# DMA chains that add up weight blocks, put at other steps of a kernel of attention and two feed-forward blocks

## The chip, the core and the metric

The kernel runs on one core of a Trainium2 chip. The metric is the device time of one execution in microseconds (us); lower is better. The engines are named as the profile names them: PE is TensorE, DVE is VectorE, ACT is ScalarE, POOL is GpSimd, SP is SyncE, which here only issues DMAs.

## What is computed

Attention over 4 batches and 12 heads, and then two feed-forward blocks on its 1792 tokens of width 768. All is float32 in the result; the five weight matrices arrive as float64.

```python
def _attn_ref(q, k, v, g_q, g_k):            # (4, 12, 448, 64)
    q_n, k_n = rmsnorm(q, g_q), rmsnorm(k, g_k)
    scores = 1.0 / np.sqrt(64) * np.matmul(q_n, k_n.transpose(0, 1, 3, 2))
    ...                                      # softmax over the keys
    return np.matmul(attn, v)

x = attn_out.transpose(0, 2, 1, 3).reshape(1792, 768)
h = 1.0 / (1.0 + np.exp(-(x @ w_gate))) * (x @ w_val)     # 768 -> 1536
y = h @ w_out                                             # 1536 -> 768
r = np.maximum(y @ w_in2, 0.0)                            # 768 -> 2048
out = (r * r) @ w_out2                                    # 2048 -> 768
```

## The kernel before

A batch is 448 tokens. The kernel has four stretches. A prologue does the attention of batch 0. **The first sweep** runs the four layers (gate and value; `w_out`; `w_in2`; `w_out2`) for batch 0 while the attention of batch 1 is done between its matmuls; in it the weights are read as float64, made float32 and written back to DRAM as blocks `w32[i]` (named `w` in the rows, 128 x 768). **The second sweep** runs the four layers for batch 1, and between them goes the attention of batches 2 and 3, twelve pairs of heads. **The joint stretch** runs the four layers for batches 2 and 3 together. Its first, third and fourth layers do a product of 2 x 2 blocks with seven block products in place of eight (`seven`), which needs sums of the blocks of the weights beside the blocks themselves.

Every weight block is loaded from DRAM into one of three buffers `wraw` (L143, L149, issued by SP), and split into a high and a low part `wsp` (four buffers) by an ACT cast (L193) and a DVE subtraction (L194); a float32 product is then three matmuls (`mm3`).

**The sums of the weights** are made by DMAs alone, in DRAM. `add_up` (L594) makes one sum in two halves: SP copies the first term to its place (L599), and later POOL adds the second term to it with an accumulating DMA (L597). A chain is three stages of such sums, in all four copies and four accumulations of 192 KB each, where a later stage copies a result of an earlier one. `pair_chains` makes the chains of the first layer (tiles `ws`, 12 chains) and of the third (tiles `wu`, 8 chains), `quad_chains` those of the fourth (tiles `wt`, 8 chains). `set_out(at, chains_, first, apart, gap)` is the table that puts them in time: half `h` of stage `n` of chain `i` is issued at step `first + apart * i + gap * (2 * n + h)`. In the second sweep a step is one of the pieces, some 2 us long, into which the sweep is cut (the sweep yields after each); in the joint stretch it is a beat, one block product of nine matmuls in the first and third layers. The joint stretch has 84 beats in the first layer, 24 in the second and 56 in the third, and whatever stands at a later beat is issued at the end of the third layer (`beat_on(30)`).

**The attention of a pair of heads in the second sweep** takes 16 or 17 pieces and starts while the pair before it is being finished: its q and k are loaded (L381, SP); DVE sums their squares (L255) and scales the sums (L260); POOL raises them to the power -1/2 (L261); DVE multiplies q and k by the result (L265, tile `qk`); PE turns them (L571, `att<-ident,qk` or `acc<-ident,qk`); ACT and DVE split them into `ks` and `qs` (L414, L415, L422, L425); SP moves halves of `qs` and `ks` to other partitions (L434, then L430); and only then can PE compute the scores (L566, `att<-ks,qs`). Behind them come the row maxima (L447), the turned probabilities (L479, L487, L491, tile `parts`) and the product with v (L566, `att<-parts,vs`). The last pieces of the sweep also split parts of the joint stretch's input (`x_part`, L638 on ACT and L639 on DVE).

PE's instructions are held in program order in these two stretches, and SP, POOL, DVE and ACT each work through one list in order. The order of those lists is made by the framework's scheduler from the program order, by its own model of time. So a step moved in the table can change the order of other instructions too. A copy or an accumulation of a chain is tied in that order to the matmul ahead of it, but does not wait for it on the chip: it waits only for its data.

Of the kernel before, what the change touches and what calls it, by code (L numbers as in the profile page):

```python
# [17 lines left out]
def attention_moe_moe2_kernel(  # L18
# [20 lines left out]
    K1 = F1 // 128  # L39
    K2 = F2 // 128  # L40
# [59 lines left out]
    K4 = K2 // 2  # L100
# [3 lines left out]
    w1s = [dram_p.tile([128, 1536], F32, tag=f"ws{p}", name=f"ws{p}") for p in range(K1)]  # L104
    w3s = [dram_p.tile([128, 1536], F32, tag=f"wu{p}", name=f"wu{p}") for p in range(K2 // 2)]
# [15 lines left out]
    W3 = 2 * K1 + 2 * KD  # L121
# [479 lines left out]
    def set_out(at, chains_, first, apart, gap):  # L601
        for i, chain in enumerate(chains_):
            for n, sums in enumerate(chain):
                for half in range(2):
                    at.setdefault(first + apart * i + gap * (2 * n + half), []).append((add_up, (sums, half)))

    beat, at_beat = [0], {}
# [7 lines left out]
    def pair_chains(i0, i1, t):  # L615
        a11, a12, a21, a22 = (w32[i][:, h:h + 384] for i in (i0, i1) for h in (0, 384))
        s = [t[:, 384 * n:384 * (n + 1)] for n in range(4)]
        return [[(s[0], a21, a22), (s[2], a11, a21)], [(s[1], s[0], a11)], [(s[3], s[1], a12)]]

    def quad_chains(kb):  # L620
        b11, b21, b12, b22 = (
            w32[W4 + K4 * hf + kb][:, 384 * r:384 * r + 384] for hf in range(2) for r in range(2))
        t = [wt[n][kb // 2][:, 384 * (kb % 2):384 * (kb % 2) + 384] for n in range(4)]
        return [[(t[0], b11, b12), (t[2], b12, b22)], [(t[1], t[0], b22)], [(t[3], t[1], b21)]]
# [76 lines left out]
    def joint():  # L701
        edge = att_tile()
        for kc in range(NF + 1):
            n = 128 if kc < NF else TAIL
            nc.tensor.transpose(edge[:n, 0, kc * QR:(kc + 1) * QR], ident[:QR, :n], ident[:QR, :QR])
        set_out(at_beat, [quad_chains(kb) for kb in range(K4)], 4, 14, 10)
        hr = one.tile([128, 27, N], F32R, tag="hr", name="h")
        rt = one.tile([128, 9, N], F32R, tag="rt", name="h")
        room = [hr[:, i] for i in range(27)] + [rt[:, i] for i in range(9)]
# [580 lines left out]
    next(pro, None)  # L1290
    def steps_of_1():
        at = {}
        set_out(at, [pair_chains(4 * (p // 2) + p % 2, 4 * (p // 2) + 2 + p % 2, w1s[p]) for p in range(K1)]
                + [pair_chains(W3 + 2 * m, W3 + 2 * m + 1, w3s[m]) for m in range(K2 // 2)], 5, 8, 8)
        order.extend(["xy1", "raw64", "raw64", "raw64", "kq", "qs", "kq", "p", "p", "pt", "p"])
        for j in range(3):
            for i, what in enumerate(("B11", "B21")):
                at.setdefault(158 + 6 * j + 3 * i, []).append((x_part, (j, what)))
        for i, what in enumerate(("sums", "B22")):
            at.setdefault(180 + 4 * i, []).append((x_part, (0, what)))  # L1300
            at.setdefault(195 + 3 * i, []).append((x_part, (1, what)))
        return at

    for s in range(2):
        slots = slots_of(s + 1)
        if s == 0:
            xtile[1] = xbuf(1)
        else:
            xwhole[0] = one.tile([128, 2, KD, N], F32, tag="xy0", name="xwhole")
        total, done = len(slots), 0  # L1310
        extra = steps_of_1() if s == 1 else {}
        for i, _ in enumerate(sweep(s)):
            if s == 0 and i == 0:
                for _ in pro:
                    pass
                continue
            fixed[0], roomy[0] = s == 1, s == 1 and i < 150
            now[0] += 1
            tick()
            for fn, args in extra.pop(i, []):  # L1320
                fn(*args)
            want = min(total, i + 1 if s == 1 else (i + 1) * total // 66)
            while done < want:
                for f in slots[done]:
                    f()
                done += 1
# [7 lines left out]
    for _ in joint():  # L1334
        pass
# [30 lines left out]
```

## Time and profile before

| what | value |
|---|---|
| median of 3 runs | 1268.12 us (1268.11 to 1270.33) |
| the profiled execution, its own time | 1264.9 us |
| span in the trace, first to last instruction | 1263.1 us |
| mean granted clock of TensorE | 0.996 of full |
| busy: PE, DVE, ACT, POOL | 98%, 75%, 63%, 18% of the span |
| second sweep and joint stretch, in the trace | about 390 to 811 us, and 811 to 1263 us |

Busy times are shares of the span; a busy PE isn't PE at its peak, since a matmul that runs at half clock is busy too. Idle time ahead of an instruction stands in brackets behind it, with what ended it.

### The profile page before, as it was taken

How to read it: one execution, taken by the hardware profiler on the slowest of the kernel's cores; microseconds unless marked ns; L12 is line 12 of the kernel's file. 1: busy time of each engine (PE TensorE's matmuls, PEld its weight loads, DVE VectorE, ACT ScalarE, POOL GpSimd, SP SyncE). 2: the span in 40 equal slices, each digit the busy share in tenths (PEclk: the TensorE clock that was granted, in tenths of full speed). 3: DMA queues.
4: the chain of work that ended last, by engine and by line, in shares of the span. 5: the costliest groups of instructions: out<-in, count | busy, mean ns of one | idle time of the engine just before them, and what ended most of it. 6: DMA issues, size and time to landing. Idle time of an engine off the chain costs nothing.

```text
span 1263.1 us, 19134 instructions
## 1 busy us (share of the span) xinstructions
PE 1234.6 (98%) x6599; PEld 1079.7 (85%) x6599; DVE 946.4 (75%) x1492; ACT 791.9 (63%) x1603; POOL 228.6 (18%) x236
## 2 busy tenths in 40 slices
PE   8999999999999999999999899999999999999998
PEld 6545788878888988898887898999999999999998
DVE  6866988778875788987887766777886336889872
ACT  5757886768765887876788665666564323335451
POOL 3301323211220222333333221001111000000000
PEclk9999999999999999999999899999999999999999
DMA  5535998998796688899899745355665334543443
GB/s 138 129 122 151 312 324 263 296 285 239 234 321 174 168 180 193 211 218 227 201 218 215 164 108 140 115 151 148 170 174 145 76 91 111 137 124 94 133 137 114
DMA packets 200545, 225.81 MB, mean 179 GB/s; under 512 B 83968, under 2 KB 178176, under 8 KB 200448
## 3 DMA queue, kind: packets, MB, share of 16 engines
q1 hardware_dynamic: 177024, 175.36, 48.1%
q0 software_dynamic: 21568, 48.77, 17.5%
q8 instruction: 52, 0.85, 0.3%
q10 hardware_dynamic: 1856, 0.46, 0.2%
q14 instruction: 45, 0.37, 0.1%
HBM read 185.99 MB, written 76.28 MB: 208 GB/s over the span
## 4 chain that ended last, share of the span: by engine, by line
PE 86%; DVE 4%; ACT 3%; DMA 3%; issue 2%; SPq 1%; POOL 0%; DVEq 0%; ACTq 0%; POOLq 0%
PE acc L566 54%; PE att L566 17%; PE att L291 3%; PE att L571 3%; DMA ks<-ks 2%; PE acc L345 2%; PE att L345 1%; PE acc L914 1%; PE acc L327 1%; PE att L327 1%; PE acc L571 1%; DVE wsp L194 1%; ACT p L458 1%; DMA out_dram<-ob 0%; ACT wsp L193 0%
## 5 line engine op out<-in xcount | busy, mean ns | idle before, releaser
L566 PE MATMUL acc<-xy,wsp 128*128 128x448 f32 x1368 | 304.9, 373 | 4.8 <-ACT wsp L193 2.7
L193 ACT CAST wsp<-wraw 128x768 fp32r<-128x768 f32 x246 | 205.8, 837 | 160.1 <-PE acc L566 72.2
L194 DVE TENSOR_TENSOR wsp<-wraw,wsp 128x768 fp32r<-128x768 f32 x246 | 235.5, 958 | 85.9 <-ACT wsp L193 83.8
L566 PEld LDWEIGHTS acc<-xy,wsp 128*128 128x128 f32 x1368 | 252.1, 189 | 35.8 <-ACT wsp L193 5.4
L566 PE MATMUL att<-parts,wsp 128*128 128x448 f32 x720 | 152.4, 365 | 0.0
L566 PEld LDWEIGHTS att<-parts,wsp 128*128 128x128 f32 x720 | 135.2, 188 | 10.8
L566 PE MATMUL acc<-parts,wsp 128*128 128x448 f32 x540 | 116.0, 365 | 0.0
L261 POOL TENSOR_TENSOR ms<-ms,mhalf 112x16 f32<-112x16 f32 (+1 forms) x25 | 81.8, 3273 | 186.6 <-DVE ms L260 174.5
L566 PE MATMUL acc<-wsp,rb 128*128 128x384 f32 x576 | 110.3, 341 | 0.0
L566 PEld LDWEIGHTS acc<-parts,wsp 128*128 128x128 f32 x540 | 101.4, 188 | 8.0
L566 PEld LDWEIGHTS acc<-wsp,rb 128*128 128x128 f32 x576 | 100.8, 190 | 2.4 <-issue 1.3
L566 PE MATMUL acc<-hb,wsp 128*128 128x448 f32 x432 | 95.1, 371 | 0.0
L566 PE MATMUL acc<-h,wsp 128*128 128x448 f32 x432 | 87.7, 365 | 0.0
L566 PEld LDWEIGHTS acc<-hb,wsp 128*128 128x128 f32 x432 | 79.3, 188 | 9.2 <-issue 2.8
L566 PEld LDWEIGHTS acc<-h,wsp 128*128 128x128 f32 x432 | 81.2, 188 | 6.4
L597 POOL DMA_DIRECT2D wt<-w x32 | 26.2, 860 | 288.8 <-DMA wt<-wt 208.3
L167 ACT ACTIVATE wraw<-raw 128x768 f32<-128x768 f32 x64 | 58.4, 914 | 27.7 <-DVE wsp L194 15.7
L182 POOL DMA_DIRECT2D w<-wraw x64 | 35.6, 556 | 205.6 <-DVE wraw L175 194.0
L458 ACT ACTIVATE p<-att,nm 112x448 f32<-112x448 f32 x96 | 60.0, 631 | 16.1 <-DVE nm L447 15.0
L309 ACT ACTIVATE p<-att,nm 112x448 f32<-112x448 f32 x88 | 55.2, 638 | 21.3 <-DVE nm L297 19.5
L566 PE MATMUL acc<-wsp,rp 128*128 128x384 f32 x360 | 64.0, 334 | 0.0
L566 PEld LDWEIGHTS acc<-wsp,rp 128*128 128x128 f32 x360 | 62.6, 188 | 0.0
(205 smaller groups left out, 2041.7 us busy)
## 6 DMA issues: line engine op xcount, KB each, us to landing
wraw<-w SPq DMA_DIRECT2D x80, 384.0 KB, 3.8
w<-wraw POOLq DMA_DIRECT2D x64, 384.0 KB, 6.3
raw<-in_moe_w_out_dram SPq DMA_DIRECT2D x28, 768.0 KB, 7.1
wraw<-w SPq DMA_DIRECT2D x92, 192.0 KB, 2.5
raw<-in_moe_w_in_dram SPq DMA_DIRECT2D x16, 768.0 KB, 5.9
raw<-in_moe_w_gate_dram SPq DMA_DIRECT2D x12, 768.0 KB, 6.4
raw<-in_moe_w_val_dram SPq DMA_DIRECT2D x12, 768.0 KB, 6.5
ws<-w POOLq DMA_DIRECT2D x48, 192.0 KB, 5.8
```

What stands on the lines that cost most here:

```text
L167: size = nc.scalar.activation(out=t, in_=hi.bitcast(F32), func=AF.Prelu, scale=2.0 ** -112, alpha=2.0 ** 32)
L182: nc.gpsimd.dma_start(out=w32[i], in_=wraw[i])
L193: nc.scalar.copy(out=sp[:, 0], in_=t)
L194: nc.vector.tensor_tensor(out=sp[:, 1], in0=t, in1=sp[:, 0].bitcast(F32), op=ALU.subtract)
L261: nc.gpsimd.tensor_tensor(out=ms, in0=ms, in1=mhalf[:QR, 0:ms.shape[1]], op=ALU.pow)
L291: nc.tensor.matmul(out=ps[:QR, e, :S], lhsT=kq[a, 1, c * QR:(c + 1) * QR], rhs=kq[a, 0], start=True, stop=True)
L309: nc.scalar.activation(out=p[:, e], in_=ps[:QR, e, :S], func=AF.Exp, bias=nm[:, e:e + 1], scale=st["rq"][:, c, e:e + 1] if "rq" in st else ...
L345: nc.tensor.matmul(out=o[e * D:(e + 1) * D], lhsT=v[:, kc, e], rhs=pt[:, (NF + 1) * e + kc if kc < NF else NF], start=(kc == 0), stop=(kc ...
L458: nc.scalar.activation(out=p[:, i * S:(i + 1) * S], in_=ps[:QR, i, :S], func=AF.Exp, bias=nm[:, i:i + 1], accum_out=su[:, c, e:e + 1])
L566: m = latest[0] = nc.tensor.matmul(**kw)
L571: m = nc.tensor.transpose(*a)
L597: held(nc.gpsimd.dma_start(out=dst, in_=second, accum_op=ALU.add))
```

## The change

Three calls of `set_out` are put differently. The eight chains of the third layer leave the second sweep, where they stood behind the twelve of the first layer, and go to the beats 2 to 104 of the joint stretch. The twelve chains that stay in the sweep begin 13 steps apart in place of 8, so that the last half stands at step 188 in place of 197 (which was a third-layer chain's). The eight chains of the fourth layer begin at beat 60 in place of 4, 13 apart in place of 14, with halves 5 beats apart in place of 10; their last half stands at beat 176 in place of 152, which is behind the 164 beats of the first three layers. No instruction is added or dropped.

```diff
@@ joint
-        set_out(at_beat, [quad_chains(kb) for kb in range(K4)], 4, 14, 10)
+        set_out(at_beat, [pair_chains(W3 + 2 * m, W3 + 2 * m + 1, w3s[m]) for m in range(K2 // 2)], 2, 11, 5)
+        set_out(at_beat, [quad_chains(kb) for kb in range(K4)], 60, 13, 5)
@@ steps_of_1
-        set_out(at, [pair_chains(4 * (p // 2) + p % 2, 4 * (p // 2) + 2 + p % 2, w1s[p]) for p in range(K1)]
-                + [pair_chains(W3 + 2 * m, W3 + 2 * m + 1, w3s[m]) for m in range(K2 // 2)], 5, 8, 8)
+        set_out(at, [pair_chains(4 * (p // 2) + p % 2, 4 * (p // 2) + 2 + p % 2, w1s[p]) for p in range(K1)], 5, 13, 8)
```

PE's list is the same in both kernels; the lists of the other engines differ at the places where chains stand, and at a few more. Three of them follow.

On DVE, in the second sweep where its fourth layer begins, the two multiplications L265 that scale q and k of the eleventh pair stand near the splits L639 of the joint stretch's input and the copies L487 and L491 of the probabilities. Before:

```order
817 L194 TENSOR_TENSOR wsp<-wraw,wsp 128x768
818 L639 TENSOR_TENSOR parts<-xwhole,parts 128x448 x3
819 L447 TENSOR_REDUCE nm<-att 112x2
820 L639 TENSOR_TENSOR parts<-xwhole,parts 128x448 x3
821 L487 TENSOR_TENSOR parts<-att,parts 128x3x224
822 L491 TENSOR_TENSOR parts<-att,parts 64x112 x2
823 L265 TENSOR_TENSOR qk<-qk,ms 112x512 x2
824 L194 TENSOR_TENSOR wsp<-wraw,wsp 128x768
```

With the change:

```order
817 L194 TENSOR_TENSOR wsp<-wraw,wsp 128x768
818 L639 TENSOR_TENSOR parts<-xwhole,parts 128x448 x3
819 L447 TENSOR_REDUCE nm<-att 112x2
820 L265 TENSOR_TENSOR qk<-qk,ms 112x512 x2
821 L639 TENSOR_TENSOR parts<-xwhole,parts 128x448 x3
822 L487 TENSOR_TENSOR parts<-att,parts 128x3x224
823 L491 TENSOR_TENSOR parts<-att,parts 64x112 x2
824 L194 TENSOR_TENSOR wsp<-wraw,wsp 128x768
```

The two L265 have moved ahead of three L639, one L487 and two L491.

On SP, in the second sweep at the fifth pair of heads, where the halves of `qs` and `ks` are moved (L434, L430) and q and k of the next pair are loaded (L381). Before:

```order
255 L149 DMA wraw<-w_137 128x768
256 L381 DMA qk<-in_k_dram 112x4x64 x2
257 L434 DMA qs<-qs 64x896 x2
258 L430 DMA ks<-ks 128x2x64
259 L381 DMA qk<-in_q_dram 112x4x64 x2
260 L149 DMA wraw<-w_138 128x768
```

With the change:

```order
247 L381 DMA qk<-in_k_dram 112x4x64 x2
248 L381 DMA qk<-in_q_dram 112x4x64 x2
249 L149 DMA wraw<-w_137 128x768
250 L434 DMA qs<-qs 64x896 x2
251 L599 DMA ws_181<-ws_181 128x384
252 L430 DMA ks<-ks 128x2x64
253 L149 DMA wraw<-w_138 128x768
```

Two loads of q and one of a weight block now stand ahead of the move of `qs`, and a copy of a chain between it and that of `ks`.

On SP, in the joint stretch late in its first layer, copies of chains (L599) among the loads of weights (L149). Before:

```order
416 L599 DMA wt_95<-w_164 128x384
417 L599 DMA wt_103<-w_172 128x384
418 L149 DMA wraw<-w_119 128x384 x2
419 L149 DMA wraw<-ws_183 128x384 x3
420 L149 DMA wraw<-w_121 128x384
421 L599 DMA wt_99<-wt_95 128x384
422 L149 DMA wraw<-ws_183 128x384
423 L149 DMA wraw<-w_120 128x384 x2
424 L149 DMA wraw<-ws_184 128x384 x3
```

With the change:

```order
430 L599 DMA wu_194<-wu_194 128x384
431 L149 DMA wraw<-w_128 128x384
432 L149 DMA wraw<-ws_188 128x384
433 L599 DMA wu_195<-wu_195 128x384
434 L149 DMA wraw<-ws_188 128x384 x2
435 L599 DMA wu_196<-w_158 128x384
436 L599 DMA wu_196<-w_157 128x384
437 L149 DMA wraw<-w_130 128x384
438 L149 DMA wraw<-ws_188 128x384
439 L599 DMA wt_95<-w_163 128x384
440 L599 DMA wt_103<-w_171 128x384
```

Where three copies stood among twelve loads of weights, six now stand among six.

## Rows read from the trace of the kernel before

**Rows 1.** Page, busy time of an engine: us, share of the span, instructions.

```profile
PE 1234.6 (98%) x6599; PEld 1079.7 (85%) x6599; DVE 946.4 (75%) x1492; ACT 791.9 (63%) x1603; POOL 228.6 (18%) x236
```

**Rows 2.** Windows: stretch, then busy us (instructions) by engine, clock, DMA share, GB/s.

```profile
400.00:800.00 400.00, 385.30 (x2147) 351.70 (x2146) 310.14 (x515) 290.31 (x653) 109.45 (x103) 0.99 0.78 183
811.00:920.00 109.00, 109.00 (x541) 101.07 (x540) 88.73 (x127) 72.22 (x128) 10.68 (x13) 1.00 0.60 158
920.00:964.00 44.00, 44.00 (x219) 40.77 (x219) 34.59 (x49) 27.85 (x50) 5.71 (x7) 1.00 0.66 169
1128.00:1154.00 26.00, 26.00 (x130) 24.10 (x129) 23.37 (x39) 11.42 (x22) 0.00 (x0) 1.00 0.35 107
```

**Rows 3.** Waits of PE, 400 to 800 us: us in total, times, longest.

```profile
PE att L571 <- issue: 3.3, 1, 3.3
PE att L566 <- DMA qs<-qs: 3.3, 2, 2.0
...
PE att L566 <- DMA ks<-ks: 1.7, 4, 0.7
```

**Rows 4.** Timeline of PE from 717 us: start, us, instructions, idle before.

```profile
717.37 1.73 PE L571 MATMUL att<-ident,qk 112*128 112x112 f32 x8 [3.29 <-issue]
718.78 3.23 PE L566 MATMUL acc<-wsp,rb 128*128 128x384 f32 x9
721.80 2.22 PE L566 MATMUL att<-parts,vs 128*128 128x448 f32 x7
```

**Rows 5.** Timeline of DVE, 711 to 718 us.

```profile
711.92 1.09 DVE L447 TENSOR_REDUCE nm<-att 112x2 f32<-112x896 f32 x1
712.92 1.68 DVE L639 TENSOR_TENSOR parts<-xwhole,parts 128x448 fp32r<-128x448 f32 x3
714.53 0.85 DVE L487 TENSOR_TENSOR parts<-att,parts 128x672 fp32r<-128x672 f32 x1
...
715.98 1.29 DVE L265 TENSOR_TENSOR qk<-qk,ms 112x512 f32<-112x512 f32 x2
```

**Rows 6.** Timeline of POOL, 700 to 712 us.

```profile
708.23 2.93 POOL L261 TENSOR_TENSOR ms<-ms,mhalf 112x16 f32<-112x16 f32 x1 [8.62 <-DVE ms L260]
```

**Rows 7.** Windows right behind that idle time, columns as in rows 2.

```profile
716.40:723.20 6.80, 5.83 (x21) 5.73 (x22) 4.09 (x8) 2.21 (x4) 0.00 (x0) 0.50 0.29 78
```

**Rows 8.** Timeline of PE at the same step of the next pair.

```profile
752.62 0.93 PE L571 MATMUL att<-ident,qk 112*128 112x112 f32 x8
753.33 1.29 PE L566 MATMUL acc<-wsp,rb 128*128 128x384 f32 x6
754.45 1.60 PE L566 MATMUL att<-parts,vs 128*128 128x448 f32 x7
```

**Rows 9.** Timeline of SP's queue, tenth pair: start, us of issuing, DMAs.

```profile
679.89 4.07 SPq L381 DMA_DIRECT2D qk<-in_q_dram  x2
684.06 2.69 SPq L434 DMA_DIRECT2D qs<-qs  x2
```

**Rows 10.** Timeline of SP's queue, fifth pair.

```profile
526.81 1.14 SPq L434 DMA_DIRECT2D qs<-qs  x2
528.65 0.64 SPq L430 DMA_DIRECT2D ks<-ks  x1
529.35 1.19 SPq L381 DMA_DIRECT2D qk<-in_q_dram  x2
```

**Rows 11.** The tile qs, 400 to 800 us: DMAs from issue to landing.

```profile
DMA to landing us min/median/max: 2.7/6.5/8.9
```

**Rows 12.** DMA queues, 400 to 800 us: packets, MB, share of 16 engines; one issue.

```profile
q0 software_dynamic: 11524, 15.75, 26.8%
...
ws<-w POOLq DMA_DIRECT2D x48, 192.0 KB, 5.8
```

**Rows 13.** Waits of SP's queue from 800 us on: total, times, longest.

```profile
SPq L149 <- DVE wsp L194: 300.4, 101, 8.2
```

**Rows 14.** Waits of ACT from 800 us on.

```profile
ACT wsp L193 <- PE att L566: 66.7, 33, 2.8
```

## The prediction

> **What bounds the kernel now.** I read the busy times first. PE is busy 1234.6 us of a span of 1263.1 [rows 1], so all that a better placing of other work can win is the 28.5 us in which PE stands, and what PE loses at half clock. Then I read where that time lies, by windows: from 400 to 800 us PE is busy 385.3 of 400 us, so 14.7 us are idle in the second sweep, while in the joint stretch it is busy in every window from 811 to 920, 920 to 964 and 1128 to 1154 us without a gap [rows 2]. The sweep can win, the joint stretch can only lose. Third, what PE waits for in the sweep: once 3.3 us ahead of the turning of q and k (L571), twice for the moved halves of `qs`, 3.3 us in all, and four times for those of `ks`, 1.7 us [rows 3]. Fourth, the timelines at these places, below.
>
> **The chains leave the sweep.** In it run 20 chains, eight DMAs each. The DMA engines are 0.78 busy on average [rows 2], and the accumulations alone take 26.8% of all 16 over 400 us [rows 12]: 107 us for 80, or 1.34 us of the whole DMA system each. With eight chains gone, 32 accumulations and 32 copies go, so at least 32 x 1.34 = 43 us, and the share falls to 0.67 or lower. A copy's price stands in no row; at 0.4 to 0.9 us, between a third and two thirds of an accumulation, the share would be 0.60 to 0.64. The wait that this shortens is that for `qs` and `ks`: a move of `qs` lands 2.7 to 8.9 us after it is issued, 6.5 in the median [rows 11], for the same 224 KB; the spread is what other DMAs cost it. I take 1.5 us off the landing.
>
> **Term A, the stop at 714 us.** PE ends its last matmul at 714.08 and begins to turn the eleventh pair's q and k at 717.37 [rows 4]. It waits for L265 on DVE, which runs from 715.98 to 717.27 [rows 5]. POOL's power, its input, was there at 711.16 [rows 6]: the data were early, and DVE's order made them late. Ahead of L265 stand three L639, L487 and two L491, from 712.92 to 715.98, 3.06 us [rows 5]. The change puts L265 ahead of them. It then runs right behind L447, from 712.92 to 714.21, and PE waits about 0.2 us instead of 3.29: **-3.1 us**. Right behind the stop the clock granted to TensorE is 0.50, its lower level of 1.2 GHz, for 6.8 us [rows 7]. From 717.37 to 724.02 PE there does eight turnings, nine matmuls with `rb` and seven with `vs` [rows 4]. The next pair's, at full clock, take 0.71, 1.12 for six with `rb` (so 1.68 for nine) and 1.60 us [rows 8], 3.99 in all against 6.65: the half clock cost **2.7 us**. PE had been idle 3.29 us before it; a stop of 2.0 us at `qs` [rows 3] was not followed by one. I count it as gone with the stop. What is late in its place is what L265 passes: the L487 and L491 of the probabilities end 1.3 us later, at 717.3, and `parts,vs` needs them. PE would come there at 714.3 + 0.71 + 1.68 = 716.7, so it may wait 0.3 to 0.6 us: **+0.3**. A is -5.5. Its bounds: -5.8, and -2.5 if the clock falls all the same. The trace shows no case of this order, so a small chance stays that L265 is late for another reason.
>
> The Trainium skill (TensorE: Matmul & The Clock Gate, HAM oscillation) takes the penalty as the throttled time times one minus the ratio of the clocks: 6.8 x 0.5 = 3.4 us, called an estimate, where the rows give 2.7. By it A would be -6.2. I keep the rows' value, since part of the 6.8 us was the end of the wait.
>
> **Term B, the tenth pair.** PE stops 2.0 us for `qs` and 0.7 for `ks` there, the longest of either row [rows 3]. SP was held: two loads of q took 4.07 us to issue, ending at 683.96, and the move of `qs` behind them took 2.69 [rows 9], where the same loads took 1.19 and the same move 1.14 at the fifth pair [rows 10]. Issuing takes longest where the DMA engines are fullest; five chains overlap there. SP's order stays, but 1.5 us off the landing and 1 us off the issue are together 2.5 of the 2.7: I take **-2.0**, bounds -2.7 and 0.
>
> **Term C, the other stop for `qs`**, 1.3 us [rows 3], at the seventh pair: one load of q, 0.6 us [rows 10], now stands behind the move instead of ahead of it, and the landing is shorter: **-1.2**, bounds -1.5 and 0. The other three stops for `ks` are 1.0 us in all, 1.7 less the 0.7 of term B [rows 3]: **-0.4**, bounds -1.0 and 0.
>
> **Term D, the fifth pair, a loss.** Ahead of the move of `qs` now stand two loads of q, 1.19 us [rows 10], and a load of a block (0.3 to 0.5 us in SP's rows); between it and that of `ks` a copy, some 0.5. The move of `ks` leaves about 2.0 us later and lands 1.0 to 1.5 sooner after its issue. PE has 0 slack there: it is one of the four places with a stop for `ks`. I take **+1.0**; bounds 0 and +2.0. At the third and sixth pair loads of k and q also come ahead of `qs`, but there two copies of chains leave the same place: nothing.
>
> **The chains in the joint stretch cost nothing** in the sum. Without chains the DMA engines are 0.35 busy (1128 to 1154), with eight DMAs in 14 beats 0.60 to 0.66 [rows 2], so a DMA a beat costs about 0.5. Third-layer chains alone, eight in 11 beats, make 0.70; where the fourth's overlap them, from beat 60 to 84 of the first layer (920 to 964 us), there are 8/11 + 8/13 = 1.34 a beat, and the share comes to about 1.0. The cover is the buffers: SP waits 300.4 us, 101 times, for a `wraw` to be free [rows 13], and ACT waits 66.7 us for a `wsp` that PE still reads [rows 14]. Loads wait for PE, not PE for loads; three `wraw` and three `wsp` ahead are about six blocks, each 3.6 us of PE. A copy that waits on SP for its accumulation holds up loads behind it; it stands 10 beats, some 18 us, behind its first copies, and copy and accumulation land 6 us each. Without the cover every late block would cost its lateness. The last chain, put behind the last beat, is issued as the fourth layer begins; its result is needed in that layer's last block.
>
> A rule that speaks against this: the Trainium skill (DMA: Bandwidth & Descriptors, Issuing engines are not separate DMA queues) says that DMAs of SP and POOL run on the same 16 engines and interleave. By it the accumulations moved to POOL's list in the joint stretch slow the weights' loads there as they slowed `qs` in the sweep; no row shows the joint stretch with 1.34 chain DMAs a beat. It is the first rival below.
>
> **Sum.** -5.5 - 2.0 - 1.2 - 0.4 + 1.0 = -8.1 us. Against the profiled execution, 1264.9, that is 1256.8; the median of the runs is 3.2 above that execution, and the same difference on 1268.1 gives **1260 us**, 0.64% faster.
>
> **Rivals.**
> 1. *The overlap starves PE (slower).* From 920 to 964 us the DMA system is full, and SP's list stands at copies that wait for accumulations. It decides from the point where loads come later than the six blocks of cover, about 20 us behind. For: 1.0 by the sum above, six copies among six loads. Against: the sweep was as full for tens of us without a wait of PE for `wsp` among its largest. Twelve blocks, each late by 1 us, are +12: 1268.1 - 8.1 + 12 = **1272 us**. Chance 0.09.
> 2. *The stops only move.* A holds, but the moves of `qs` and `ks` gain nothing in sum, since SP's new order (term D) gives back what the emptier queues win: -5.5, **1262.6 us**. Chance 0.15.
> 3. *L265 comes no earlier on the chip, or the clock falls all the same.* Then A is between 0 and -2.5, and with B, C and D at -2.6 the time is 1263 to **1265.5 us**. Chance 0.16, a third of it within 0.2%.
> 4. *Nothing that counts.* A fails and the stops only move: **1268 us**. Chance 0.08.
>
> **How the numbers follow.** The forecast has 0.52. 0.2% is 2.5 us, about what a measurement of this kernel tells from no change. Faster by more: the forecast, rival 2 and two thirds of rival 3, 0.52 + 0.15 + 0.11 = 0.78; I say 0.76, since one run in the three shown stands 2.2 us off. Same: 0.15. Slower: 0.09. The likeliest case's own range, with its bounds for B, C and D, is 1256.5 to 1263.5. The range that holds 8 in 10 reaches from all stops gone and D at zero (-5.8 - 2.7 - 1.5 - 1.0 = -11.0, or 1257.1, and 1.5 for the runs' spread) to rival 4: 1255.5 to 1268.5.
>
> **What would show it.** A: no idle time over 0.6 us ahead of the eleventh pair's turning, and a granted clock of 1.00 behind it. B and C: waits of PE for `qs` under 1 us in all, median landing of `qs` near 5 us, a DMA share of 0.60 to 0.67 from 400 to 800 us. D: a stop for `ks` of 0.5 to 2 us at the fifth pair. Joint stretch: PE busy without a gap, a DMA share near 1.0 from beat 60 to 84. The prediction is wrong if PE stands in the joint stretch, or if stops for `qs` or `ks` grow at several pairs, or one of them lets the clock fall.

## The result, and the profile after

The change takes **1256.49 us** in the median (1255.81 to 1258.56, 4 runs) where the kernel before took 1268.11 (1266.41 to 1270.33, 4 runs): a ratio of 0.991, 95% interval 0.9891 to 0.993, so 11.6 us or 0.9% faster. Forecast were 1260.0 us, with 1255.5 to 1268.5 as the range. The direction and the range held, the gain is 3.5 us larger than the 8.1 of the sum, and its parts are not those of the sum. The profiled execution took 1255.81 us, its span is 1254.0.

The windows come first, as in [rows 2]: stretch, busy us (instructions) of PE, PEld, DVE, ACT and POOL, granted clock, DMA share, GB/s.

```profile
400.00:800.00 400.00, 391.74 (x2213) 360.15 (x2212) 319.62 (x531) 296.07 (x663) 82.48 (x71) 1.00 0.63 153
811.00:920.00 109.00, 109.00 (x539) 101.01 (x538) 87.21 (x122) 70.64 (x125) 18.97 (x23) 1.00 0.76 188
920.00:964.00 44.00, 44.00 (x219) 40.77 (x218) 33.51 (x49) 25.35 (x44) 11.66 (x15) 1.00 0.89 225
1128.00:1154.00 26.00, 26.00 (x137) 24.74 (x136) 25.46 (x43) 14.23 (x29) 2.44 (x3) 1.00 0.60 149
```

In the sweep PE is idle 8.3 of 400 us where it was 14.7, at full clock, and the DMA share is 0.63. In the joint stretch the DMA engines now carry 0.76 and 0.89 in place of 0.60 and 0.66, and PE still stands nowhere. What PE waits for from 400 to 800 us (in total, times, longest) answers to [rows 3]:

```profile
PE att L571 <- ACT p L458: 2.3, 1, 2.3
PE att L566 <- DVE ks L425: 2.1, 2, 1.1
PE acc L571 <- DVE qk L265: 1.8, 1, 1.8
```

All six waits for the moved halves of `qs` and `ks` are gone. A stop of 2.3 us ahead of the turning of q and k is left, but another line ends it, and a second wait of 1.1 us for `ks` (for its subtraction on DVE, not its move) stands in the list. The moves land sooner, as the tile `qs` shows (against [rows 11]), and the software queue of the accumulations takes 17.1% of the DMA engines against [rows 12]:

```profile
DMA to landing us min/median/max: 2.8/5.0/6.8
...
q0 software_dynamic: 6942, 9.53, 17.1%
```

**Where the time came from.** PE's list is the same in both kernels, so the start of the same instruction can be subtracted. Four rows of PE's timeline of the kernel before, each with the idle time ahead of it in brackets:

```profile
460.50 0.99 PE L571 MATMUL acc<-ident,qk 112*128 112x112 f32 x8 [1.79 <-DVE qk L265]
619.30 1.49 PE L566 MATMUL acc<-xy,wsp 128*128 128x448 f32 x6 [0.24 <-ACT rl L977]
681.94 1.48 PE L566 MATMUL acc<-xy,wsp 128*128 128x448 f32 x6 [0.37 <-ACT rl L977]
774.89 0.47 PE L566 MATMUL att<-parts,vs 128*128 128x448 f32 x1 [1.88 <-DVE parts L639]
```

And the same four in the change:

```profile
462.23 0.98 PE L571 MATMUL acc<-ident,qk 112*128 112x112 f32 x8 [1.79 <-DVE qk L265]
618.43 1.50 PE L566 MATMUL acc<-xy,wsp 128*128 128x448 f32 x6 [0.26 <-ACT rl L978]
679.98 1.48 PE L566 MATMUL acc<-xy,wsp 128*128 128x448 f32 x6 [0.37 <-ACT rl L978]
765.76 0.47 PE L566 MATMUL att<-parts,vs 128*128 128x448 f32 x1 [0.24 <-ACT p L458]
```

The differences are +1.73, -0.87, -1.96 and -9.13. The first comes from the prologue, ahead of anything that the change touches (there the profiled execution of the change ran 6.8 us at half clock near 18 us); taken off, the change gains 2.6 us by the second row, 3.7 by the third and 10.9 by the last. Subtracting all 6599 matmuls in this way gives -0.7 at the fifth pair of heads, -1.8 at the seventh, -1.1 at the ninth, -3.2 at the tenth, -2.3 at the eleventh, -1.6 at the twelfth, and from there to the end, the whole joint stretch through, a constant -10.84. (Small drifts make up the rest.)

The gain of a pair is 0.35 to 0.6 us more than its stops were: 3.2 at the tenth for stops of 2.02 and 0.68, 1.8 at the seventh for 1.42. Two stops break the four matmuls of the scores into two twos, as the tenth pair of the kernel before shows:

```profile
693.06 0.62 PE L566 MATMUL att<-ks,qs 128*112 128x448 f32 x2 [2.02 <-DMA qs<-qs]
694.36 0.66 PE L566 MATMUL att<-ks,qs 128*112 128x448 f32 x2 [0.68 <-DMA ks<-ks]
```

Two and two take 1.28 us; four without a stop between them take 1.04 to 1.05 (below), so about 0.25 of it comes of the break, and counts as busy.

**The eleventh pair**, where term A lay. PE of the change, to be read beside [rows 4]:

```profile
711.20 0.98 PE L571 MATMUL att<-ident,qk 112*128 112x112 f32 x8 [2.31 <-ACT p L458]
711.95 1.82 PE L566 MATMUL acc<-wsp,rb 128*128 128x384 f32 x9
713.61 1.60 PE L566 MATMUL att<-parts,vs 128*128 128x448 f32 x7
715.05 1.21 PE L566 MATMUL acc<-wsp,rb 128*128 128x384 f32 x6
717.33 1.04 PE L566 MATMUL att<-ks,qs 128*112 128x448 f32 x4 [1.07 <-DVE ks L425]
```

On DVE L265 has moved as the lists said, and is done 2.2 us before PE begins:

```profile
707.72 1.28 DVE L265 TENSOR_TENSOR qk<-qk,ms 112x512 f32<-112x512 f32 x2
```

PE stands all the same, 2.31 us of the 3.29, until ACT has read the scores of the pair before (L458) out of the PSUM bank into which the turning writes. ACT's timeline says why that is late: six splits L638 stand ahead of it.

```profile
703.96 2.91 ACT L638 CAST parts<-xwhole 128x448 fp32r<-128x448 f32 x6
...
709.80 0.64 ACT L458 ACTIVATE p<-att,nm 112x448 f32<-112x448 f32 x1
...
710.95 0.20 ACT L458 ACTIVATION_READ_ACCUMULATOR p<-att,nm 112x1 f32 x1
```

The kernel before had this wait too, hidden: there the last of L458 ended less than 1 us ahead of L265.

```profile
716.14 0.20 ACT L458 ACTIVATION_READ_ACCUMULATOR p<-att,nm 112x1 f32 x1
```

That is 716.34 for ACT and 717.27 for DVE [rows 5], both after 714.08, when PE was free: so of the 3.29 us of idle time DVE's order alone could win 1.0. Nor did the half clock of [rows 7] come back as a whole: behind the stop of 2.31 us the clock stays at full, but a stop of 1.07 us for `ks` comes 6 us later, which in the kernel before the slow stretch had covered.

### The profile page after: what moved, and what is told of

Its sections match the earlier page's. It is cut to its first block, busy times and chain, and to the rows that moved or that the text cites. A ratio compares the mean times of both kernels' runs of the same rounds, so it can differ in the third digit from the quotient of the medians.

```text
span 1254.0 us, 19116 instructions
## 1 busy us (share of the span) xinstructions
PE 1232.8 (98%) x6599; PEld 1077.7 (86%) x6599; DVE 946.7 (75%) x1492; ACT 791.7 (63%) x1603; POOL 225.9 (18%) x236
## 4 chain that ended last, share of the span: by engine, by line
PE 89%; DVE 4%; ACT 4%; DMA 2%; issue 1%; SPq 1%; DVEq 0%; ACTq 0%
PE acc L566 57%; PE att L566 18%; PE att L291 3%; PE att L571 3%; PE acc L345 2%; PE att L345 2%; PE acc L915 1%; PE acc L571 1%; PE acc L327 1%; DMA raw<-in_moe_w_gate_dram 1%; PE att L327 1%; DVE wsp L194 1%; ACT p L309 0%; ACT p L458 0%; ACT wsp L193 0%
## 5 line engine op out<-in xcount | busy, mean ns | idle before, releaser
L566 PE MATMUL acc<-xy,wsp 128*128 128x448 f32 x1368 | 304.5, 372 | 5.3 <-ACT wsp L193 3.1
L193 ACT CAST wsp<-wraw 128x768 fp32r<-128x768 f32 x246 | 205.7, 836 | 158.5 <-PE acc L566 71.4
L194 DVE TENSOR_TENSOR wsp<-wraw,wsp 128x768 fp32r<-128x768 f32 x246 | 235.5, 958 | 83.9 <-ACT wsp L193 81.8
L566 PEld LDWEIGHTS acc<-xy,wsp 128*128 128x128 f32 x1368 | 251.7, 189 | 36.1 <-ACT wsp L193 5.6
L566 PE MATMUL att<-parts,wsp 128*128 128x448 f32 x720 | 152.5, 365 | 0.0
L566 PEld LDWEIGHTS att<-parts,wsp 128*128 128x128 f32 x720 | 135.1, 188 | 10.8
L566 PE MATMUL acc<-parts,wsp 128*128 128x448 f32 x540 | 116.0, 365 | 0.0
L566 PE MATMUL acc<-wsp,rb 128*128 128x384 f32 x576 | 108.9, 338 | 0.0
L566 PEld LDWEIGHTS acc<-parts,wsp 128*128 128x128 f32 x540 | 101.3, 188 | 8.0
L566 PEld LDWEIGHTS acc<-wsp,rb 128*128 128x128 f32 x576 | 99.6, 188 | 2.4 <-issue 2.0
L566 PE MATMUL acc<-hb,wsp 128*128 128x448 f32 x432 | 95.1, 371 | 0.0
L566 PE MATMUL acc<-h,wsp 128*128 128x448 f32 x432 | 87.7, 365 | 0.0
L566 PEld LDWEIGHTS acc<-hb,wsp 128*128 128x128 f32 x432 | 79.3, 188 | 9.2 <-issue 2.7
L566 PEld LDWEIGHTS acc<-h,wsp 128*128 128x128 f32 x432 | 81.1, 188 | 6.4
L458 ACT ACTIVATE p<-att,nm 112x448 f32<-112x448 f32 x96 | 60.1, 631 | 18.1 <-DVE nm L447 17.1
L566 PE MATMUL acc<-wsp,rp 128*128 128x384 f32 x360 | 64.0, 334 | 0.0
L566 PEld LDWEIGHTS acc<-wsp,rp 128*128 128x128 f32 x360 | 62.6, 188 | 0.0
L175 DVE SCALAR_TENSOR_TENSOR wraw<-wraw,raw 128x768 int32<-128x768 int32 x64 | 60.8, 954 | 0.8
```

The costliest lines, as they stand in the source:

```text
L175: nc.vector.scalar_tensor_tensor(out=ti, in0=ti, scalar=3, in1=hi, op0=ALU.logical_shift_left, op1=ALU.bitwise_or)
L193: nc.scalar.copy(out=sp[:, 0], in_=t)
L194: nc.vector.tensor_tensor(out=sp[:, 1], in0=t, in1=sp[:, 0].bitcast(F32), op=ALU.subtract)
L458: nc.scalar.activation(out=p[:, i * S:(i + 1) * S], in_=ps[:QR, i, :S], func=AF.Exp, bias=nm[:, i:i + 1], accum_out=su[:, c, e:e + 1])
L566: m = latest[0] = nc.tensor.matmul(**kw)
```

## The experiments

The kernel before ran again beside them, 17 times with the first four (median 1266.89 us, 1264.89 to 1272.34) and 23 times with the last four (1266.98, 1261.35 to 1273.24).

**1. The third layer's chains moved, the twelve not spread.** The change with the first-layer chains 8 steps apart as before.

```diff
-        set_out(at, [pair_chains(...) for p in range(K1)], 5, 13, 8)
+        set_out(at, [pair_chains(...) for p in range(K1)], 5, 8, 8)
```

> The change, but the twelve first-layer chains stay 8 steps apart, so that they are as dense as before up to step 133 (about 650 us) and gone behind it. Theory (the load that the chains put on the DMA engines makes the moves of qs and ks late): as dense as before, the stops come back where they stood in the dense stretch, about 0.3 us at the fifth pair and 1.4 us at the seventh, and stay away at the ninth and tenth, behind the chains; median landing of qs between 5.0 and 6.5 us; 1 to 2 us slower than the change, 1257.5 to 1258.5 us. Rival (it is enough that the eight third-layer chains left): no stop for qs or ks anywhere, the time of the change, 1256.5 us.

It took 1259.35 us (6 runs; ratio to before 0.9931, interval 0.9913 to 0.995). In its trace nothing is won as far as 650 us, where its chains stand as thick as before, then 1.0 us at the ninth pair, 3.2 at the tenth, 2.3 at the eleventh and 2.7 at the twelfth. Three stops for moves are left, at the fifth and the seventh pair: `PE att L566 <- DMA ks<-ks: 1.2, 2, 0.7`, and one of 0.94 us that the profile gives to DVE's L194, though the moved half of `qs` lands 0.14 us before PE begins there. So the places at which stops vanish are those from which chains are taken. By the subtraction of starts these places win 9.2 us. The whole trace wins 7.6, because the clock fell for 3.4 us behind the stop of 1.79 us near 461 us, which cost 1.6; experiment 8, whose chains stand in the sweep as in the change, has the same fall at the same cost, so it is not the price of the dense chains. What spreading the twelve wins is what is missing at the fifth and the seventh pair, 1.1 and 1.8 us (at the twelfth this run wins 1.1 more than the change). The medians differ by 2.9 us, with intervals that overlap.

**2. The fourth layer's table alone.** The kernel before with that one call.

```diff
-        set_out(at_beat, [quad_chains(kb) for kb in range(K4)], 4, 14, 10)
+        set_out(at_beat, [quad_chains(kb) for kb in range(K4)], 60, 13, 5)
```

> The kernel before with the change to the fourth layer's chains alone (beat 60, 13 apart, 5 between halves). Theory (all of the gain lies in the second sweep): the stops of 3.3 us ahead of the turning and of 5.0 us at qs and ks stay, PE has no gap in the joint stretch, 1268 us within 2 us. Rival (the joint stretch gained too): 2 us faster or more.

It took 1267.97 us (12 runs; 1.0001, 0.9985 to 1.0017): nothing, and every stop of the sweep is there (`qs` 4.1 us, the eleventh pair's 3.3, `ks` 2.0). This part of the change only makes room.

**3. The splits of the input tied to their step.** `held` binds L638 and L639 of the `x_part` steps to the matmul ahead of them in the program, in the lists of ACT and DVE; no wait is added.

```diff
+        both = (nc.scalar.copy(out=hi, in_=src),
+                nc.vector.tensor_tensor(out=lo, in0=src, in1=hi.bitcast(F32), op=ALU.subtract))
+        if tie:
+            for one_of in both:
+                held(one_of)
```

> The change, and the six splits of the joint stretch's input near 710 us (L638 on ACT, L639 on DVE) are tied to the matmul at their step instead of running in a bunch as soon as they may. Theory (the 2.3 us that PE still stands ahead of the eleventh pair's turning are a wait for the scores' bank, which ACT reads late because six L638, 2.9 us, stand ahead of it): the stop falls to under 0.5 us, what follows it (1.1 us for ks) stays or grows by up to 1 us; 1 to 2.5 us faster than the change, 1254 to 1255.5 us. Rival (the stop is DVE's or POOL's): it stays above 2 us, 1256.5 us.

It took 1253.18 us (5 runs; 0.9881, 0.9864 to 0.9897). Against the change that is 3.3 us by the medians and 1.6 by the starts of the two traces, where 2.4 are won at the eleventh pair and the rest is lost again elsewhere. The stop there is gone altogether, while the later one for `ks` stays:

```profile
709.76 0.98 PE L571 MATMUL att<-ident,qk 112*128 112x112 f32 x8
715.89 1.05 PE L566 MATMUL att<-ks,qs 128*112 128x448 f32 x4 [1.05 <-DVE ks L425]
```

So what was late at the eleventh pair, on ACT as on DVE, were splits that the order of the lists had put ahead of work that PE wanted sooner.

**4. DVE's old order put back.** The change, with L265 of the eleventh pair tied behind the splits L639 and the copies L487 and L491, as the kernel before had it; PE's and ACT's lists stay, and SP's but for one copy of a chain. (A helper of three lines shifts the line numbers by a few.)

```diff
+        for after in (behind if (st["b"], st["hp"]) == (3, 2) else []):
+            tc.add_manual_dep(
+                hat.ins, after.ins.name,
+                mybir.DependencyInfo(mybir.DependencyClass.NoSync, mybir.DependencyReason.SCHED_ONLY), reason="order")
...
-                at.setdefault(158 + 6 * j + 3 * i, []).append((x_part, (j, what)))
+                at.setdefault(158, []).append((x_part, (j, what)))
```

> The change, with DVE's order around the eleventh pair's L265 put back as it was before (behind three L639, L487 and two L491); the chains stand as in the change. Theory of two waits at one place (L265 and the scores' bank): the stop is 3.3 us again, 1.0 more than in the change, the clock falls behind it for some 6.8 us, 2.7 us, and the 1.1 us for ks go under in that; 2.5 to 3.5 us slower than the change, 1259 to 1260 us. Rival 1 (the prediction's term A): 5.5 us slower, 1262 us. Rival 2 (the clock does not hang on this stop): 0 to 1 us slower, clock 1.00 throughout.

It took 1256.19 us (6 runs; 0.9904, 0.9887 to 0.9922), 0.3 below the change. The old stop is back in full:

```profile
709.95 1.18 PE L578 MATMUL att<-ident,qk 112*128 112x112 f32 x8 [3.29 <-issue]
```

and the clock falls behind it, for 3.4 us this time. But the stop of 1.07 us for `ks` behind it is gone in return: 3.29 against 2.31 and 1.07. By the starts the old order loses 1.2 us to the change at the eleventh pair, and wins 1.1 at the twelfth, where the change's small stops of 0.24 and 0.32 us are absent. (It loses another 1.9 in the third layer of the joint stretch, where its matmuls follow one another some 2% more slowly without a stop; why stays open.) In the medians of the whole kernel DVE's order, on which term A rested, is worth nothing that these runs can measure, and the 2.5 to 3.5 us of this theory did not come.

**5. The tied splits on the kernel before.** The edit of experiment 3, the chains where they were.

> The kernel before, with its chains where they were, and only the splits of the joint stretch's input (L638 on ACT, L639 on DVE) put back in the lists to the step at which the program has them, so that neither DVE's L265 nor ACT's reading of the scores' bank (L458) stands behind them. Theory: the stop of 3.3 us at the eleventh pair had two waits, one under the other, and both came from these splits. Then the whole stop and the half clock behind it go, -3.1 and -2.7 as in term A, and the stop of 1.9 us at the twelfth pair behind the same splits perhaps too: 1261 to 1264 us, while the stops for qs (3 to 4 us in all) and ks stay, with a median landing of qs of 6 to 7 us. Rival: the stop is DVE's order alone, and the run with the old order showed that it is worth about nothing: 1266 to 1269 us.

It took 1264.62 us (12 runs; 0.9979, 0.9959 to 0.9999). In the profiled execution, which was the fastest of the twelve, the stop shrinks to 1.42 us, the profile names another line for its end once more, and the clock stays at full.

```profile
711.56 0.96 PE L571 MATMUL att<-ident,qk 112*128 112x112 f32 x8 [1.42 <-ACT wsp L193]
717.66 1.04 PE L566 MATMUL att<-ks,qs 128*112 128x448 f32 x4 [1.05 <-DVE ks L425]
```

The name is wrong, as the two engines show:

```profile
709.94 0.83 ACT L193 CAST wsp<-wraw 128x768 fp32r<-128x768 f32 x1
710.17 1.29 DVE L265 TENSOR_TENSOR qk<-qk,ms 112x512 f32<-112x512 f32 x2
```

L193 had ended at 710.77, 0.79 us before PE begins, and L458 ahead of it at 710.05. L265 ends at 711.46, 0.10 us before PE begins, just as in the kernel before (717.27 and 717.37). So it is the first wait again: the splits are gone from ahead of L265, but one L487 and two L491 still stand there. The runs together make a table of the two waits:

| L265 on DVE | the splits L638 on ACT | stop of PE | runs |
|---|---|---|---|
| behind L639, L487, L491 | six ahead of L458 | 3.29 us | before, experiments 2 and 4 |
| ahead of L487 and L491 | six ahead of L458 | 2.31 us | the change, 1 and 8 |
| behind L487 and L491 | at their steps | 1.42 us | 5 |
| ahead of L487 and L491 | at their steps | none | 3 and 7 |

(Experiment 6, whose lists of ACT and DVE differ at this place, has 1.55 us.) The place of L265 alone leaves 2.31 us, that of the splits alone, on both engines, 1.42, and the two together nothing. The subtraction of starts gives 4.7 us in this execution, the medians 2.4. The stop for `qs` (2.9 us in all) and the median landing of `qs` (6.5 us) are those of the kernel before, so these stops have nothing to do with the splits.

**6. The load put back without the chains.** The change with 64 copies of 192 KB on POOL's queue at the steps where the third layer's chains stood. Nothing reads them, and SP's and PE's lists are those of the change (ACT's and DVE's differ around the eleventh pair).

```diff
+    def spare_copy(m, n):
+        held(nc.gpsimd.dma_start(
+            out=spare[n // 2][:, 384 * (n % 2):384 * (n % 2) + 384], in_=w32[W3 + 2 * m + n % 2][:, 0:384]))
...
+        for m in range(K2 // 2):
+            for n in range(8):
+                at.setdefault(5 + 8 * (K1 + m) + 8 * (n // 2) + 8 * (n // 4), []).append((spare_copy, (m, n)))
```

> The change, with 64 copies of 192 KB from DRAM to DRAM put on POOL's queue at the second sweep's steps at which the third layer's chains stood before; nobody reads them. SP's and PE's lists are those of the change. It adds transfers that the change doesn't have, as many as it took out. Theory (the stops for qs and ks are set by what else the DMA engines carry): the DMA share of 400 to 800 us goes back from 0.63 to 0.70 or more, the median landing of qs from 5.0 to 6 us or more, stops of PE for qs or ks of 2 us or more come back, and the time is 1259 to 1262 us, 3 to 5 above the change. Rival (SP's order and its waits set them, not the load): stops for qs and ks stay under 0.5 us in all and the time is within 1.5 us of the change, 1255 to 1258 us.

It took 1266.11 us (12 runs; 0.9993, 0.9976 to 1.0009): the whole gain is gone. The DMA share from 400 to 800 us is 0.71, as expected; the median landing of `qs` is 5.4 us, short of the 6 expected. The stops are back:

```profile
PE att L566 <- DMA qs<-qs: 4.3, 2, 2.9
...
PE att L571 <- DVE xwhole L524: 1.7, 1, 1.7
PE att L566 <- DMA ks<-ks: 1.7, 2, 0.9
```

At the tenth pair two moves of `qs` take 3.09 us to issue in place of 1.20, and at the ninth and tenth they land after 8.7 to 12.5 us. The start of the matmuls falls back by 2.7 us between 654 and 677 us and by 7.3 at the tenth pair, where the clock also falls for 3.4 us. The fifth and the seventh pair, ahead of the first copy (594.7 us), keep what they had won. At the ninth and tenth pairs SP's order is thus not what the change gains by: the load is. (At the fifth and seventh experiment 1 changes the load and SP's list together, so there the two are not told apart.) Not all of the 9.6 us is load, though, and the loss is larger than the 3 to 5 us expected. The copies come in a denser burst, and the stops of the tenth pair, 2.89 and 0.86 us, are longer than in the kernel before. The clock falls near 461 us, ahead of the copies, which costs 1.7. And the wait for L524 is longer by 1.4 us because ACT's and DVE's lists differ there: two casts of `r` now stand ahead of ACT's L517, which L522 and then L524 need, and L447 stands ahead of L524 on DVE.

**7. The best of it.** The kernel of experiment 3, with DVE's L265 of the third pair tied ahead of the L487 and L491 that it stood behind.

```diff
+            hat = first[0]
+            first.clear()
+            tc.add_manual_dep(
+                part.ins, hat.ins.name,
+                mybir.DependencyInfo(mybir.DependencyClass.NoSync, mybir.DependencyReason.SCHED_ONLY), reason="order")
```

> The change with the tied splits of the joint stretch's input, and with DVE's L265 of the third pair put ahead of the L487 and L491 that it stood behind. Theory: the stop of 1.8 us for L265 at about 460 us goes as well and PE gains it whole: about 1.5 us under the tied kernel's 1253.2, so 1251 to 1252.5 us. Rival: another wait lies under this one as well, as at the eleventh pair, and the time stays at 1253 to 1254 us.

It took 1251.73 us (6 runs, 1249.38 to 1253.32; 0.9876, 0.9851 to 0.9902), 1.2% under the kernel before. PE waits 0.4 us for L265 in place of 1.8:

```profile
PE att L578 <- DVE ks L429: 2.2, 2, 1.1
PE att L578 <- ACT p L462: 0.8, 1, 0.8
...
PE acc L583 <- DVE qk L267: 0.4, 1, 0.4
```

Here no other wait of that size lay under the one removed; the subtraction of starts gives 1.2 us at that place against experiment 3. The median is 1.5 us below that of experiment 3, with intervals that overlap, so the whole kernel alone doesn't show the gain.

**8. The joint stretch pushed.** The change with both joint tables as dense as their chains allow, which puts the first rival to the test.

```diff
-        set_out(at_beat, [pair_chains(W3 + 2 * m, W3 + 2 * m + 1, w3s[m]) for m in range(K2 // 2)], 2, 11, 5)
-        set_out(at_beat, [quad_chains(kb) for kb in range(K4)], 60, 13, 5)
+        set_out(at_beat, [pair_chains(W3 + 2 * m, W3 + 2 * m + 1, w3s[m]) for m in range(K2 // 2)], 2, 4, 5)
+        set_out(at_beat, [quad_chains(kb) for kb in range(K4)], 2, 4, 5)
```

> The change, with both tables of the joint stretch as dense as their chains allow: the third layer's eight chains begin 4 beats apart in place of 11, the fourth's eight at beat 2 and 4 apart in place of beat 60 and 13 apart. All 128 DMAs are then issued in some 60 beats, over two a beat. It asks how much the joint stretch's buffers cover, the first rival of the prediction. Theory: the cover is large; the DMA share from 811 to 920 us goes to 0.95 or more, PE stands for wsp or wraw less than 3 us in all, 1256 to 1260 us. Rival: with more DMA work than the stretch can carry PE stands for the weights, 1265 us or more.

It took 1282.59 us (4 runs; 1.0124, 1.0089 to 1.0159), the rival's side of the expectation. Windows of its joint stretch:

```profile
811.00:840.00 29.00, 29.00 (x145) 26.87 (x144) 21.13 (x30) 15.69 (x29) 11.60 (x14) 1.00 1.05 268
840.00:861.00 21.00, 19.29 (x95) 17.22 (x94) 9.45 (x13) 11.21 (x21) 8.25 (x10) 1.00 1.10 255
861.00:885.00 24.00, 18.05 (x74) 15.53 (x72) 14.88 (x22) 8.22 (x14) 11.59 (x14) 0.86 1.13 275
885.00:911.00 26.00, 17.87 (x73) 14.16 (x72) 15.40 (x23) 11.88 (x22) 9.96 (x13) 0.93 1.12 280
```

With the DMA share over 1.0 (packets overlap in the count) PE runs 29 us on its buffers, and then stands some 16 of 71, and loses the clock besides. Behind it ACT waits for blocks, and the loads land after 8.8 us in the median where the change's land after 2.9:

```profile
ACT wsp L193 <- DMA wraw<-ws: 29.7, 9, 7.0
ACT wsp L193 <- DMA wraw<-w: 21.5, 6, 6.9
```

The rule that the prediction weighed (the Trainium skill, DMA: Bandwidth & Descriptors, Issuing engines are not separate DMA queues: DMAs share the same 16 engines whichever engine issues them) agrees with this run and with experiment 6, where copies on POOL's queue made moves on SP's late by several us. It did not decide the change itself, whose share stays at 0.89.

## Why the prediction was right in sum and wrong in its parts

- **The chains leave the sweep: right.** A DMA share of 0.60 to 0.67 and a median landing near 5 us were forecast; 0.63 and 5.0 came. Experiments 1, 2 and 6 show that it is this load that the stops hung on.
- **Term A, -5.5: wrong, and the step that failed is "PE waits about 0.2 us instead of 3.29": PE waited 2.31.** L265 came when forecast, but under its wait lay that for ACT's L458, which the profile of before doesn't list: it gives the whole stop to one name, "issue" [rows 3]. Measured are -2.3 at this place: 1.0 of idle time and 2.7 or less of half clock, less 1.07 and the break that it makes for `ks`, which the slow stretch had hidden. DVE's order accounts for about half of that: with the old order 1.2 of it was lost, and the rest was that the clock fell for 3.4 us there and not for 6.8 (experiment 4). The whole stop goes only when the splits leave ACT's list as well (experiments 3 and 5). The +0.3 for `parts` did not appear.
- **Term B, -2.0: mis-sized, -3.2.** The whole stop of 2.7 us went, and with it the broken run of the scores' matmuls. The loads of q and the moves behind them, 4.07 and 2.69 us to issue in [rows 9], took 1.53 and 1.20.
- **Term C and the other stops for `ks`, -1.6 together: mis-sized, -3.6** (seventh, fifth and ninth pair: 1.8, 0.7, 1.1). The stops went whole, where I had let a remainder stand.
- **Term D, +1.0: wrong.** SP's order at the fifth pair is as forecast, and yet its small stop is gone too. The timeline of SP there:

```profile
525.73 1.10 SPq L381 DMA_DIRECT2D qk<-in_q_dram  x2
526.92 0.44 SPq L149 DMA_DIRECT2D wraw<-w  x1
528.00 1.25 SPq L434 DMA_DIRECT2D qs<-qs  x2
529.34 0.54 SPq L599 DMA_DIRECT2D ws<-ws  x1
530.05 0.99 SPq L430 DMA_DIRECT2D ks<-ks  x1
```

  And DVE's, which writes what is moved:

```profile
527.29 1.40 DVE L422 SCALAR_TENSOR_TENSOR qs<-acc,gains,qs 64x448 fp32r<-64x448 f32 x2
528.73 1.26 DVE L425 TENSOR_TENSOR ks<-acc,ks 64x448 fp32r<-64x448 f32 x2
```

  SP is done with the loads at 527.36, 0.64 us before the move of `qs` begins, and that begins as the first of the two L422 ends, halfway through their 1.40 us; the move of `ks` begins as the second L425 ends, at 529.99. I had put SP's issue times one behind the other as if `qs` were ready before them; it wasn't, so they cost nothing. The moves landed after 4.0 and 3.3 us.
- **Not foreseen, -1.6 at the twelfth pair.** In the kernel before PE stood 1.88 us there. The profile names a split L639 on DVE, but ACT's last L458, which every other trace with this stop except experiment 5's names, ended at 774.84, 0.05 us before PE begins. L458 needs L447, and that stands in DVE's list behind L653, which begins as a store of `out_dram` lands:

```profile
771.72 0.62 DVE L653 TENSOR_TENSOR t<-t,xwhole 128x448 f32<-128x448 f32 x1 [1.79 <-DMA out_dram<-ob]
774.64 0.20 ACT L458 ACTIVATION_READ_ACCUMULATOR p<-att,nm 112x1 f32 x1
```

  The longest landing of these stores from 740 to 800 us and PE's stop go together in all ten traces: 6.3 us and 1.88 before, 5.8 and 1.34 in experiment 5, 5.3 and 0.89 in 2, 5.1 and 0.81 in 7, 4.6 to 4.7 and 0.24 to 0.37 in the change, 3 and 6, 4.4 and 0.04 in 8, and 2.5 and 3.9 without a stop in 1 and 4. The cause, a store slowed by chains, is argued from these pairs; no run changes the store alone. In the profile of before it is 1.9 us, the third largest of PE's waits in the sweep, and I did not cost it.
- **The joint stretch at nothing: right.** The lag is constant through it. Experiment 8 shows that the cover was real and finite, and that the rival had the right mechanism and the wrong point: not 0.89 of the DMA engines, forecast as about 1.0, but more than 1.0 for longer than some 30 us.
- **The sum.** Terms of -2.3, -3.2, -3.6, 0 and -1.6 make -10.7 against the 10.84 of the traces and the 11.6 of the medians. An overestimate of 3.2 in A was more than paid for by what B, C, D and the twelfth pair gave. That the total came within 3.5 us of the sum is in good part luck: the errors had opposite signs. One figure beside the sum doesn't follow from its terms either: with A at -5.5 the bounds of B, C and D span 1257.4 to 1264.6, not 1256.5 to 1263.5; the measured time lies 0.9 us below the first.

What stays open is how much of the gain is clock. The times of one kernel go with its mean granted clock: of 23 executions of the kernel before, the fastest (1261.35 us) had 0.997 and the slowest (1273.24) 0.988, and a straight line through them gives 1.2 us for each 0.001. The kernel of experiment 7 has 0.996 to 1.000. Fewer stops may make fewer falls, but one profile of each kernel doesn't show which stop each fall belongs to.

## What to carry to other kernels

A wait in a profile is the last of several, and the name that the profile gives it can be that of a line done long before (L193 in experiment 5): look for what ended within a tenth of a microsecond of the start. Before an edit that hurries its releaser is given the whole stop, look up when each other input and the buffer that the instruction writes came free, and credit only the distance to the next one. Transfers that nobody waits for are not free where others are waited for; put them where the loads have buffers ahead, and count the DMA share there, since 0.89 cost nothing and 1.1 cost 26 us. Where stops for transfers hang on the load, all of them, also ones at other lines, shrink together, so count every wait in the stretch that a DMA ends directly or one step behind.

## What the runs showed of the hardware

The fall of the clock behind the same stop is not the same each time. Behind the stop of 3.29 us at the eleventh pair the granted clock was 0.50 for 6.8 us in the kernel before, and for 3.4 in experiments 2 and 4. Behind the stop of 1.79 us for L265 near 461 us it fell for 3.4 us in experiments 1, 6 and 8, and not at all in the kernel before, the change, and experiments 2 to 5. Behind the tenth pair's stops it stayed up in the kernel before, where they are 2.02 and 0.68 us, and fell for 3.4 us in experiment 2, where they are 1.61 and 0.54, the shorter ones. A stop's length alone doesn't say whether a fall follows. Near 461 us, where the change has the same stop without a fall, the fall of 3.4 us cost experiments 1, 6 and 8 1.6 to 1.7 us by the subtraction of starts, as much as most of the stops studied here.
